# A fused attention, MLP and top-1 expert kernel: the first expert's rows from six gathered tiles and three tiles put to their slots by products, two low weight halves made later, another issue table

## The chip, the cores and the metric

The kernel runs on one core of one Trainium2 chip. The metric is device time in microseconds for one execution, lower is better. The runs shown are the median of three, with the lowest and the highest.

## The reference

```python
def _attn_ref(q, k, v, w1, b1, w2):            # B, H, S, D = 2, 8, 576, 64
    scores = scale * np.matmul(q, k.transpose(0, 1, 3, 2))
    x = (np.log1p(np.abs(rel)) / np.log1p(np.maximum(pos[:, None], 1.0)))[..., None]
    bias = np.maximum(x @ w1 + b1, 0.0) @ w2    # 32 hidden units, one bias per head
    attn = softmax(scores + bias.transpose(2, 0, 1)[None])
    return np.matmul(attn, v)

def _moe_ref(x, w_in, w_out):                   # x 1152x512, w_in 512x2048, w_out 2048x512
    h = x @ w_in
    return (h * np.tanh(np.log1p(np.exp(h)))) @ w_out

def _moe2_ref(x, w_gate, w1, w2, capacity):     # 8 experts, 512 -> 1024 -> 512, capacity 288
    expert_idx = np.argmax(x @ w_gate, axis=1)
    gate_w = softmax(x @ w_gate)[np.arange(N), expert_idx]
    # tokens go to their expert in the order of their numbers, until its 288 slots are full
    h = np.maximum(np.einsum('ecd,edf->ecf', disp, w1), 0.0)
    y = np.einsum('ecf,efd->ecd', h, w2)
    # out[i] = gate_w[i] * y[expert_idx[i], pos[i]] for the tokens kept, else 0
```

## The kernel before, in words

The program has two phases. **Phase 1** computes attention, the dense MLP and the gate. The 1152 tokens (2 batches of 576) are cut into five row tiles: `it` = 0 to 3 hold 128 rows of each batch (token tiles t = 0 to 7, two for each `it`), and `it` = 4 holds the 64 rows that are left of each batch (t = 8). For each row tile the scores, the bias of the relative positions, the exponentials and the product with v give the input planes PX of the MLP; `mlp_a` (products at L835 into banks of two hidden blocks, the gate function and its f16 high and low planes, L849 and L850) and `mlp_b` (products at L868, for `it` = 4 at L872) give y. Products of float accuracy are made of three f16 products: high by high, high by low, low by high.

`emit_y(it)` follows: `y_out` normalizes y (L942, L950), stores it to a scratch array `yscr` in memory, transposes it and makes the gate's logits (L964, L969); `rank_of` makes the argmax, the token's rank within its expert (one-hot rows o3, a product with a triangle at L1040) and writes token and weight to the slot table `tbl` by an indirect DMA on POOL (L1054). `slots(t)` adds one-hot rows times token numbers into `acc`, from which the rows of the first expert are read.

The first expert is the expert of token 0, known early, so that it needs no table: `first_rows` (after `it` = 3) turns `acc` into row numbers gid (L1133 to the tensor_scalar behind it), gathers the rows of the first expert from `yscr` in three groups of 96 slots (L1144, POOL) and splits them in f16 planes (L1148 high, L1149 low). `first_loads` loads its weights, measures their size and makes the f16 halves of W1 in four chunks (L1277 high, a L310 row with tile W low). `first_slots` puts rows to their slots by products: a diagonal dg moves the gathered rows (L1180), a marker tile of t = 8 moves the last tile's rows straight from the chip (L1184), for four column blocks and two planes, eight banks in all; each is cast to xT (L1186). 22 products that nobody reads stand ahead of them (L1170).

Nothing in phase 1 is issued where it is written. Each operation is recorded by `op(engine, cost, function, reads, writes, alternatives)`, and the table `ORDER` lists the operations by number (times 8, plus the way: an operation that may go to ScalarE or VectorE is sent to one of them by it). Buffers of the shared rings (R2: ra and rw, RB: pb and ps) are chosen when an operation is issued. DMAs go out on SP's queue in that order, indirect ones on POOL's. Each engine works off its own queue in order.

**Phase 2** is written in its order: `experts_list` (VectorE, list of the experts that have tokens), `gemm1(0)` and then, for each expert k, `gemm2(k)`, `gemm1(k + 1)`. `gemm1` makes eight hidden blocks ft, 12 products each (4 chunks ct by 3 planes, L1443), in four banks; each bank is taken by a Relu to the high plane HH (L1444, ScalarE) and a subtraction to the low plane (a L310 row with HH, VectorE); for ft = 2 to 5 the halves of W2 are made between them (L1427 and a L310 row with tile W). `gemm2` makes four blocks dt of 24 products (L1480) in two banks PY; between them stand the squares of the next expert's weights (L1213), their sum (L1216) and its f16 halves, and the next expert's rows, gathered at L1409. L307, L310, L313 and L327 are helpers (tensor_scalar, scalar_tensor_tensor, a scaled activation, a reduction) that many operations use.

## Time and profile before

| | us |
|---|---|
| median of the runs (n = 3) | 535.68 |
| lowest, highest | 534.3, 538.29 |
| the profiled execution | 534.81 |
| its span in the trace | 532.9 |

Its mean granted clock is 0.969 of full speed. TensorE is busy for 92% of the span, VectorE for 81%, ScalarE for 74%. The span is what lies between the first and the last instruction of the profiled execution; the time of the execution is 1.9 us longer. Times in a timeline are in us from the start of the span. PE is the matmul engine (TensorE), PEld its weight loads, DVE VectorE, ACT ScalarE, POOL GpSimd, SP the engine that issues most DMAs. PEclk is the clock that TensorE was granted, as a share of its full one. In a timeline row, what stands in brackets is how long the engine stood idle before the row, and what ended that.

### The profile page before, as it was taken

Reading aid. Unit: us, or ns where it says so; the run is one execution under the profiler, and the core shown is the slowest. Engines: PE = TensorE matmul, PEld = TensorE weight load, DVE = VectorE, ACT = ScalarE, POOL = GpSimd, SP = SyncE. Lnnn points to the kernel's source line nnn. Section 1 sums busy time; section 2 is a strip of 40 time slices with the busy share of each in tenths; the row PEclk is TensorE's granted clock in tenths of the full one; section 3 lists DMA queues with packets and bytes.
Section 4 is the critical chain, followed back from the end, with each engine's and each line's share of the span. In section 5 each row is a group of like instructions: output and inputs, shape, how many; then the busy total and the mean of one; then the engine's idle time right before and its main releaser. Section 6 shows DMA issues by size and latency. Waiting matters only on the chain.

```text
span 532.9 us, 11895 instructions
## 1 busy us (share of the span) xinstructions
PE 492.6 (92%) x4479; PEld 335.6 (63%) x4479; DVE 432.4 (81%) x1171; ACT 394.2 (74%) x808; POOL 37.8 (7%) x67
## 2 busy tenths in 40 slices
PE   4856988999999999999999999999999699999995
PEld 3411655676767674456687855899558478787551
DVE  7989899999987899999878874689988885869300
ACT  7989999999876899999996753366873357868210
POOL 1000010000000011000000000001001311212101
PEclk9896699999999999999999999999999899999999
DMA  8998787630010132346540112063001347695100
GB/s 313 414 366 293 234 290 260 228 129 1 12 63 1 66 132 68 112 152 211 169 122 5 50 35 58 21 230 128 2 26 47 105 134 237 218 342 188 42 15 19
DMA packets 28211, 73.78 MB, mean 138 GB/s; under 512 B 4838, under 2 KB 4966, under 8 KB 26096
## 3 DMA queue, kind: packets, MB, share of 16 engines
q1 hardware_dynamic: 26576, 69.21, 37.5%
q0 software_dynamic: 1568, 3.72, 2.4%
q8 instruction: 37, 0.61, 0.5%
q14 instruction: 30, 0.25, 0.2%
HBM read 55.27 MB, written 17.87 MB: 137 GB/s over the span
## 4 chain that ended last, share of the span: by engine, by line
PE 57%; DMA 19%; DVE 13%; ACT 7%; issue 3%; POOL 0%; SPq 0%; POOLq 0%; DVEq 0%; ACTq 0%
PE pb L868 16%; PE pb L835 12%; DMA out<-OC,tid 10%; PE pb L727 6%; DMA xg<-yscr,gid 6%; PE ps L835 6%; PE pb L663 3%; DMA rw<-wi 3%; PE pb L518 3%; PE ps L633 3%; PE ps L663 2%; ACT ra L655 2%; DVE rw L310 2%; ACT ra L666 2%; DVE rw L307 1%
## 5 line engine op out<-in xcount | busy, mean ns | idle before, releaser
L835 PEld LDWEIGHTS <-WIt 128*128 128x128 f16 x960 | 85.2, 98 | 10.6 <-issue 1.0
L835 PE MATMUL pb<-PX,WIt 128*128 128x256 f16 (+1 forms) x648 | 69.0, 263 | 0.0
L868 PE MATMUL pb<-WOt,ra 128*128 128x512 f16 x204 | 48.1, 379 | 0.0
L518 PE MATMUL pb<-ra,w2s 128*32 128x512 f32 (+17 forms) x252 | 37.0, 519 | 8.4 <-ACT rbe L532 3.7
L868 PE MATMUL pb<-WOt,rw 128*128 128x512 f16 x180 | 42.0, 380 | 0.0
L655 ACT ACTIVATE ra<-ra,rm 128x576 f32<-128x576 f32 x50 | 39.2, 788 | 2.2 <-DVE rm L654 1.8
L507 ACT ACTIVATE ra<-AT,stab 128x512 f32<-128x512 f32 (+17 forms) x62 | 38.4, 658 | 2.1 <-DVE stab L307 2.0
L310 DVE SCALAR_TENSOR_TENSOR W<-AT,wsc,W 128x1024 f16<-128x1024 f32 x24 | 30.5, 1279 | 6.1 <-ACT W L1427 5.8
L868 PEld LDWEIGHTS <-ra 128*128 128x128 f16 x204 | 19.8, 98 | 22.2 <-issue 0.9
L1443 PEld LDWEIGHTS <-W 128*128 128x128 f16 x288 | 28.1, 98 | 8.9 <-DVE W L310 1.2
L654 DVE CUSTOM_DVE_ANT_0 ra<-ps,ra 128x576 f32<-128x576 f32 x43 | 31.4, 753 | 2.7 <-PE ps L622 1.6
L727 PE MATMUL pb<-ra,AT 128*64 128x128 f32 (+1 forms) x540 | 32.7, 272 | 0.7 <-ACT ra L666 0.7
L835 PE MATMUL ps<-PX,WIt 128*128 128x256 f16 (+1 forms) x312 | 32.8, 260 | 0.0
L868 PEld LDWEIGHTS <-rw 128*128 128x128 f16 x180 | 17.3, 98 | 20.4 <-issue 1.4
L727 PEld LDWEIGHTS pb<-ra,AT 128*64 128x64 f32 x540 | 28.0, 139 | 3.3 <-issue 1.5
L532 ACT ACTIVATE rbe<-pb,rl 128x48 f32<-128x48 f32 (+25 forms) x64 | 28.5, 481 | 2.1 <-DMA bscr<-rbe 1.4
L1054 POOL DMA_INDIRECT tbl<-pk,rm x9 | 11.2, 1244 | 264.9 <-DVE rm L1051 175.8
L310 DVE SCALAR_TENSOR_TENSOR rw<-rw 128x1024 int32<-128x1024 int32 x24 | 29.1, 1215 | 0.0
L663 PE MATMUL pb<-ident,ra 128*128 128x128 f32 x159 | 24.0, 286 | 3.3 <-ACT ra L655 2.7
L666 ACT COPY ra<-pb 128x384 f32<-128x384 f32 x49 | 22.5, 492 | 3.5 <-PE pb L663 2.9
L1480 PE MATMUL py<-HH,W 128*128 128x288 f16 x192 | 24.7, 286 | 0.0
L307 DVE TENSOR_SCALAR ra<-AT,stab 128x544 f32<-128x544 f32 (+16 forms) x56 | 23.1, 443 | 0.9 <-PE pb L868 0.8
(477 smaller groups left out, 1151.7 us busy)
## 6 DMA issues: line engine op xcount, KB each, us to landing
AT<-m SPq DMA_DIRECT2D x24, 512.0 KB, 5.5
bscr<-rbe SPq DMA_DIRECT2D x36, 295.5 KB, 3.2
rw<-wo SPq DMA_DIRECT2D x8, 1024.0 KB, 5.4
ra<-bscr SPq DMA_DIRECT2D x28, 288.0 KB, 4.4
rw<-wi SPq DMA_DIRECT2D x4, 1024.0 KB, 9.2
WOt<-wi SPq DMA_DIRECT2D x4, 1024.0 KB, 8.5
AT<-k SPq DMA_DIRECT2D x4, 576.0 KB, 6.2
out<-ra SPq DMA_DIRECT2D x9, 256.0 KB, 2.6
```

Of the source, the lines that this page charges most:

```text
L307: eng.tensor_scalar(out=out, in0=in0, scalar1=s1, scalar2=s2, op0=op0, op1=op1)
L310: (eng or dve).scalar_tensor_tensor(out=out, in0=in0, scalar=s, in1=in1, op0=op0, op1=op1)
L507: on_act = lambda h_=h_, g=g: act.activation(h_.t[:, 0:dn], T[:, 0:dn], AF.Relu, bias=stab[:, g:g + 1])
L518: pe.matmul(ps.t[32 * c:32 * c + 32, 0:d1 - d0], w2s, hs[c].t[:, d0:d1], start=True, stop=True)
L532: op("ACT", c_act(n, 1, 50), lambda ends=ends: act.activation(*ends(), AF.Copy, scale=rl[:, blk:blk + 1]), r=[ps, "stab"], p=[be], alt=[(" ...
L654: op("DVE", c_dve(S), lambda i=i, own=own, m_=m_, b_=b_: dve.tensor_tensor_reduce(out=own(), in0=blk(s_.t[:, 960 * i:960 * i + S]), in1=bl ...
L655: op("ACT", c_act(S, 2), lambda i=i, m_=m_, col=col: act.activation(t_.t[:, S * i:S * i + S], t_.t[:, S * i:S * i + S], AF.Exp, bias=m_.t[ ...
L663: pe.transpose(pa.t[:, P * j:P * j + P], t_.t[:, 384 * n + P * j:384 * n + P * j + P], ident)
L666: op("ACT", c_act(384, 0, 55), lambda dst=dst, src=src: act.copy(dst(), src()), r=[pa], w=[("tT", it, ct, b, n)], hold=[t_], alt=[("DVE", ...
L727: pe.matmul(ov[64 * i:64 * i + 64, ct % 2, w * bb:w * bb + w], v_, t_.t[:, at + c0:at + c0 + w], start=n == 0, stop=n == 4)
L835: pe.matmul(ps.t[:, n * f_:n * f_ + n], WI[:, wv, ct, P * ft:P * ft + P], xt.t[:, xv, ct, 0:n], start=i == 0, stop=i == 11)
L868: pe.matmul(y_.t, gv()[:, g2, c:c + P], WO[:, wv, ft], **kw)
```

## The change

1. Another `ORDER`, with nine operations more.
2. The first expert's gather uses token tiles 0 to 5 alone: `first_rows` stands behind `it` = 2, and the count of rows goes over six tiles. Slots of t = 6 and 7 are not added to `acc`.
3. Tiles 6 and 7 (`it` = 3) get f16 planes on the chip (`planes`: a cast on ScalarE or VectorE and a subtraction on VectorE, L932 and L933), and their stores to `yscr` wait for the three gathers. Their rows and those of tile 8 are put to their slots by products with marker tiles m6, m7, m8: 24 products of 288 columns (L1199) instead of 8, besides the 24 of 96 columns with the diagonal (L1207). m7 takes in n0, the number of batch 0's rows in tiles 6 and 8, so one product and one VectorE operation more. `yscr` is zeroed where the gather may read rows not yet written.
4. 12 products that nobody reads (L1193) instead of 22, which wait for other things.
5. The low halves of W1's chunks 2 and 3 are made in phase 2, behind `experts_list`.
6. `gemm1(0)`: six banks (PH, PT and PY, those of the second product); 10 of 12 products of hidden blocks 0 to 5 first, without the low halves 2 and 3, then the two that are left of each, with Relu and subtraction behind each block; blocks 6 and 7 whole. For k > 0 the order is as before but for the loop's form.

```diff
@@ y_out
-            dma(lambda: yscr[t0:t0 + P], yv, 262144, r=[y_], p=["yscr"])
+            dma(lambda: yscr[t0:t0 + P], yv, 262144, r=[y_] + ([("g0", c) for c in range(NCH)] if it == NIT - 1 else []), p=["yscr"])
...
+            if it == NIT - 1:
+                planes(y_, yv)
@@
+    def planes(y_, yv):
+        h_ = pl.buf(R2)
+        hv = lambda v: h_.t.bitcast(F16)[:, DM * v:DM * v + DM]
+        op("ACT", c_act(DM), lambda: act.copy(hv(0), yv()), r=[y_], w=[h_], alt=[("DVE", c_dve(DM, 0.52), lambda: dve.tensor_copy(hv(0), yv()), 1)])
+        op("DVE", c_dve(DM), lambda: dve.tensor_tensor(out=hv(1), in0=yv(), in1=hv(0), op=ALU.subtract), r=[y_], w=[h_], lk=1)
+        yx.append((h_, hv))
@@ emit_y
-        if it == NIT - 1:
+        if it == NIT - 2:
             first_rows()
@@ first_slots
         def unread():
-            for i in range(22):
+            for i in range(12):
                 pe.matmul(pz.t[:, 0:SL], one, sl16, start=True, stop=True)
...
+                put = lambda i, m_, ps=ps, cc=cc, v=v: pe.matmul(ps.t[:, 0:SL], yx[i][1](v)[:, cc], m_.t.bitcast(F16)[:, 0:SL], start=i == 0, stop=i == 2)
+
+                def early(put=put):
+                    put(0, m6)
+                op("PE", 125, early, r=[yx[0][0], m6], w=[ps])
+
+                def f(ps=ps, cc=cc, v=v, put=put):
                     for c in range(NCH):
...
+                    put(1, m7)
...
+                op("PE", 125, lambda put=put: put(2, m8), r=[yx[2][0], m8], w=[ps])
@@ first_loads
-            op("DVE", c_dve(F2, 1.04, 1), lambda i=i, hi=hi: stt(W[1][:, 1, i], R1[:, i], sc(), hi(), ALU.mult, ALU.subtract), r=["W1", "R1", ("size", 0), ("W1h", i)], w=[("W1l", i)], lk=1)
+            if i < 2:
...
@@ gemm1
-        for ft in range(8):
-            ps = (PH + PT)[ft % 4]
-            for i, (ct, wv, xv) in enumerate([(ct, wv, xv) for ct in range(4) for wv, xv in P3]):
-                pe.matmul(ps[:, 0:SL], W1[:, wv, ct, P * ft:P * ft + P], XT[k % 2][:, xv, ct], start=i == 0, stop=i == 11)
+        banks = PH + PT if k else PH + PT + PY
...
+        ahead = 0 if k else len(banks)
+        for ft in range(ahead):
+            first(ft, [(ct, wv, xv) for wv, xv in P3 for ct in range(4) if not wv or ct < 2], True, False)
+        for ft in range(8):
+            ps = banks[ft % len(banks)]
+            if ft < ahead:
+                first(ft, [(ct, 1, 0) for ct in (2, 3)], False, True)
+            else:
+                first(ft, [(ct, wv, xv) for ct in range(4) for wv, xv in P3], True, True)
             act.activation(HH[:, 0, ft], ps[:, 0:SL], AF.Relu)
@@ phase 2
     experts_list()
...
+    for i in 2, 3:
+        stt(W1[:, 1, i], raw(0, i), sca(0, 0, 5), W1[:, 0, i], ALU.mult, ALU.subtract)
```

On POOL, the end of phase 1: the gathers of the first expert's rows (yscr, gid) among the writes of the slot table (tbl; pk_158 to pk_166 are tiles 0 to 8). Before:

```order
L1054 DMA tbl<-pk_163,rm_124 2304x2
L1054 DMA tbl<-pk_164,rm_123 2304x2
L1054 DMA tbl<-pk_165,rm_117 2304x2
L1144 DMA rw_105<-yscr,gid_183 96x512
L1144 DMA ra_112<-yscr,gid_183 96x512 x2
L1054 DMA tbl<-pk_166,rm_126 2304x2
```

And now:

```order
L1063 DMA tbl<-pk_163,rm_123 2304x2
L1160 DMA rw_105<-yscr,gid_183 96x512 x2
L1160 DMA ra_114<-yscr,gid_183 96x512
L1063 DMA tbl<-pk_164,rm_127 2304x2
L1063 DMA tbl<-pk_165,rm_118 2304x2
L1063 DMA tbl<-pk_166,rm_126 2304x2
```

The three gathers have moved ahead of the table writes of tiles 6 and 7.

On VectorE, the end of phase 1, up to the casts of the slots (xT) and the first operation of experts_list (A from cnt). W_4566 is W1 in f16, sl the slot numbers, rm a tile's slots. Before:

```order
L1149 TENSOR_TENSOR ra_109<-ra_112,ra_109 96x512
L307 TENSOR_SCALAR rm_126<-rm_126,e0s 128x1
L307 TENSOR_SCALAR rw_105<-sl_173,rm_126 128x288
L310 SCALAR_TENSOR_TENSOR W_4566<-AT,wsc,W_4566 128x1024 x2
L1186 CAST xT_4560<-pb_142 128x288
L1186 CAST xT_4560<-pb_141 128x288
L1186 CAST xT_4560<-ps_3923 128x288
L1186 CAST xT_4560<-pb_144 128x288
L307 TENSOR_SCALAR A<-cnt 1x8
```

And now, from the diagonal (ident, smsk) and m7 (with n_180) on:

```order
L1183 TENSOR_TENSOR ra_114<-ident,smsk 96x288
L1367 COPY cnt<-ps_3826 1x8
L307 TENSOR_SCALAR rw_105<-sl_173,rm_127,n_180 128x288
L310 SCALAR_TENSOR_TENSOR ra_111<-pb_143,rw_104,ra_111 128x512
L307 TENSOR_SCALAR rm_126<-rm_126,e0s 128x1
L307 TENSOR_SCALAR rw_106<-sl_173,rm_126 128x288
L1211 CAST xT_4517<-ps_3826 128x288
L1211 CAST xT_4517<-pb_141 128x288
L1211 CAST xT_4517<-pb_144 128x288
L1211 CAST xT_4517<-ps_3824 128x288
L307 TENSOR_SCALAR A<-cnt 1x8
```

The two low halves between the marker of tile 8 and the casts are gone, and so are the planes of the gathered rows; the marker m7 and tile 8's low plane stand there.

On VectorE, the start of phase 2, from the end of experts_list (lst) on; HH are the low planes of the hidden blocks by their banks, the W tile of the HH rows (W_5211, W_5181) is W2. Before:

```order
L1370 CAST lst<-fl 1x10
L307 TENSOR_SCALAR hm<-tok 96x1 x2
L310 SCALAR_TENSOR_TENSOR HH<-ph_5215,HH 128x288
L310 SCALAR_TENSOR_TENSOR HH<-ph_5216,HH 128x288
L310 SCALAR_TENSOR_TENSOR HH<-pt_5221,HH 128x288
L310 SCALAR_TENSOR_TENSOR W_5211<-AT,wsc,W_5211 128x1024
```

And now:

```order
L1396 CAST lst<-fl 1x10
L307 TENSOR_SCALAR hm<-tok 96x1 x2
L310 SCALAR_TENSOR_TENSOR W_4523<-AT,wsc,W_4523 128x1024 x2
L310 SCALAR_TENSOR_TENSOR HH<-ph_5185,HH 128x288
L310 SCALAR_TENSOR_TENSOR HH<-ph_5186,HH 128x288
L310 SCALAR_TENSOR_TENSOR HH<-pt_5191,HH 128x288
L310 SCALAR_TENSOR_TENSOR W_5181<-AT,wsc,W_5181 128x1024
```

The two low halves of W1 (W_4523) stand between the list of experts and the first low plane.

## Rows read from the trace of the kernel before

**Rows 1.** Windows by stage: length, busy PE, PEld, DVE, ACT, POOL, PEclk, DMA, GB/s.

```profile
0.00:103.30 103.30, 78.17 (x692) 44.37 (x693) 95.52 (x214) 96.46 (x193) 5.10 (x36) 0.88 0.83 298
103.30:397.60 294.30, 293.24 (x2797) 202.77 (x2794) 255.71 (x712) 232.19 (x496) 8.96 (x8) 1.00 0.25 84
397.60:412.90 15.30, 14.33 (x244) 13.22 (x243) 12.80 (x70) 5.83 (x13) 1.94 (x2) 1.00 0.19 63
412.90:429.30 16.40, 11.10 (x98) 7.77 (x98) 14.99 (x51) 6.24 (x14) 4.51 (x4) 0.79 0.29 85
429.30:441.10 11.80, 11.78 (x97) 9.42 (x98) 9.67 (x34) 7.01 (x11) 2.78 (x3) 1.00 0.57 190
441.10:455.40 14.30, 14.21 (x122) 11.60 (x119) 8.02 (x19) 12.33 (x21) 1.20 (x1) 1.00 0.78 243
```

**Rows 2.** ACT by line and shape, 0 to 101.6 us: count, busy us, mean ns, idle.

```profile
L655 ACT ACTIVATE ra<-ra,rm 128x576 f32<-128x576 f32 x19 | 15.2, 805 | 1.4 <-DVE rm L654 1.3
L666 ACT COPY ra<-pb 128x384 f32<-128x384 f32 x24 | 11.3, 506 | 0.0
...
L757 ACT ACTIVATE rw<-rw 128x1024 f32<-128x1024 f32 x4 | 4.7, 1185 | 0.0
...
L655 ACT ACTIVATION_READ_ACCUMULATOR ra<-ra,rm 128x1 f32 x19 | 4.2, 223 | 0.0
...
L532 ACT ACTIVATE rbe<-pb,rl 128x512 f32<-128x512 f32 x4 | 2.7, 680 | 0.0
...
L313 ACT ACTIVATE PX<-ra,xin 128x256 f16<-128x256 f32 x4 | 2.1, 530 | 0.0
```

**Rows 3.** Timeline, gate of tile 8 to t0: start us, us, engine, line, operation, tiles.

```profile
415.47 0.17 DVE L993 TENSOR_REDUCE rr<-pb 128x1 f32<-128x8 f32 x1
...
417.31 4.53 PE L1170 MATMUL pb<-sl,one 128*128 128x288 f16 x22
...
420.96 0.40 DVE L1148 CAST rw<-rw 96x512 f16<-96x512 f32 x1
421.40 0.69 DVE L1149 TENSOR_TENSOR rw<-rw,rw 96x512 f16<-96x512 f32 x1
...
425.12 0.29 DVE L307 TENSOR_SCALAR rw<-sl,rm 128x288 f16<-128x288 f16 x1
425.33 2.47 DVE L310 SCALAR_TENSOR_TENSOR W<-AT,wsc,W 128x1024 f16<-128x1024 f32 x2
```

**Rows 4.** Windows of the slot products' stretch, columns as in rows 1.

```profile
418.00:419.00 1.00, 1.00 (x6) 0.63 (x5) 1.00 (x1) 1.00 (x2) 0.79 (x1) 0.50 0.56 139
...
422.00:424.00 2.00, 0.25 (x2) 0.15 (x2) 1.86 (x8) 0.00 (x0) 0.00 (x0) 1.00 0.35 78
...
425.00:426.00 1.00, 0.99 (x13) 0.99 (x14) 0.96 (x3) 0.00 (x0) 0.00 (x0) 0.50 0.89 342
```

**Rows 5.** Timeline behind t0, columns as in rows 3.

```profile
429.32 3.11 PE L1443 MATMUL ph<-xT,W 128*128 128x288 f16 x24 [0.68 <-DVE A L307]
...
431.12 0.41 ACT L1444 ACTIVATE HH<-ph 128x288 f16<-128x288 f32 x1 [2.31 <-PE ph L1443]
...
432.05 0.19 DVE L307 TENSOR_SCALAR hm<-tok 96x1 f32<-96x1 int32 x2
...
434.25 1.14 ACT L1427 ACTIVATE W<-AT,wsc 128x1024 f16<-128x1024 f32 x1
...
435.42 1.28 DVE L310 SCALAR_TENSOR_TENSOR W<-AT,wsc,W 128x1024 f16<-128x1024 f32 x1 [0.58 <-ACT W L1427]
...
441.09 6.04 PE L1480 MATMUL py<-HH,W 128*128 128x288 f16 x48
...
441.44 0.81 DVE L310 SCALAR_TENSOR_TENSOR HH<-pt,HH 128x288 f16<-128x288 f32 x2
```

**Rows 6.** One line, the gathers L1144: durations in ns, and issue to landing.

```profile
L1144 POOL DMA_INDIRECT ra<-yscr,gid x2: 918/1288/1657, 417.0 to 418.2; - x2
...
DMA to landing us min/median/max: 3.0/3.6/3.8
```

More of the change, by code (lines that the diff above doesn't have):

```diff
@@ L1062, in emit_y @@
         for t, _ in rs:
-            m_ = slots(t)
-        if it == NIT - 1:
+            sm.append(slots(t))
+        if it == NIT - 2:
             first_rows()
@@ L1115, in f @@
             for b in range(2):
-                for t in range(b, 8, 2):
-                    pe.matmul(pn.t[:, E * b:E * b + E], one, o3[:, t, 1], start=t == b, stop=t == b + 6)
-        op("PE", 320, f, r=["rc0", "rc1"] + [("oh", t) for t in range(8)], w=[pn])
+                for t in range(b, 6, 2):
+                    pe.matmul(pn.t[:, E * b:E * b + E], one, o3[:, t, 1], start=t == b, stop=t == b + 4)
+        op("PE", 240, f, r=["rc0", "rc1"] + [("oh", t) for t in range(6)], w=[pn])
         def f():
@@ L1439, in gemm1, with first @@
             gather(k + 1)
-        for ft in range(8):
-            ps = (PH + PT)[ft % 4]
-            for i, (ct, wv, xv) in enumerate([(ct, wv, xv) for ct in range(4) for wv, xv in P3]):
-                pe.matmul(ps[:, 0:SL], W1[:, wv, ct, P * ft:P * ft + P], XT[k % 2][:, xv, ct], start=i == 0, stop=i == 11)
+        banks = PH + PT if k else PH + PT + PY
+        def first(ft, seq, a_, b_):
+            for i, (ct, wv, xv) in enumerate(seq):
+                pe.matmul(banks[ft % len(banks)][:, 0:SL], W1[:, wv, ct, P * ft:P * ft + P], XT[k % 2][:, xv, ct], start=a_ and i == 0, stop=b_ and i + 1 == len(seq))
+        ahead = 0 if k else len(banks)
+        for ft in range(ahead):
+            first(ft, [(ct, wv, xv) for wv, xv in P3 for ct in range(4) if not wv or ct < 2], True, False)
+        for ft in range(8):
+            ps = banks[ft % len(banks)]
[3 more added lines that the diff above has]
+                first(ft, [(ct, wv, xv) for ct in range(4) for wv, xv in P3], True, True)
             act.activation(HH[:, 0, ft], ps[:, 0:SL], AF.Relu)
```

48 lines of the change are left out of this document (29 added, 19 removed), and 218 rows, old and new, of the table ORDER.

## The prediction

> **What bounds the kernel now.** I read the windows by stage first [rows 1]. The reader is to see five different limits. Up to 103.3 us VectorE (95.5 us busy) and ScalarE (96.5) are full and TensorE, 78.2 busy, waits for them: the start is bounded by the work that these two have ahead of the first dense products. From 103.3 to 397.6 TensorE is busy for 293.2 of 294.3 us, so nothing done on another engine in that stretch moves the end, unless it stops TensorE. From 397.6 to 412.9 TensorE still has 14.3 of 15.3 us of products of the last row tile, with the gates of tiles 6 and 7 between them. From 412.9 to 429.3 it has 11.1 of 16.4 us, much of that products that nobody reads, at a mean granted clock of 0.79, while VectorE is busy for 15.0: this is the gate of the last tile and the filling of expert 0's slots, and VectorE leads. From 429.3 to 455.4 TensorE is full again (11.78 of 11.8, 14.21 of 14.3): expert 0's two products and expert 1's preparation.
>
> So three places can move the end: when the dense products start, how long it takes from the last tile's gate to the first product of expert 0 (I call that moment t0; before it is 429.32), and whether TensorE still goes without a pause from t0 on. I then read the sums by shape on ScalarE ahead of the first dense products [rows 2], the timeline from the gate to t0 [rows 3], the clock in single microseconds [rows 4] and the timeline behind t0 [rows 5].
>
> **The start.** The new table changes what stands ahead of the first tile's last input plane. Counted in the order of both kernels up to that plane, ScalarE has one exponential more (0.805 us, and its accumulator read of 0.22), one more of the 1024-wide quantizing activations L757 (1.19), about 0.85 more of bias evictions L532 (one of 352 and one of 191 columns for one of 16; I scale from 0.68 for 512 columns), two high planes less (2 x 0.53 = 1.06) and two copies L666 less (1.01); the L507 tiles are others of the same kind, +0.3 [rows 2]. That is 0.3 + 1.0 + 1.2 + 0.85 - 1.06 - 1.01, about +1.3 us on an engine that is busy for 96.5 of 103.3 [rows 1]. VectorE gets about +0.7. I take +1.3 us for the start. What the trace can't show is how the new order meshes: ScalarE idles 6.8 us in that stretch, and if half of this is saved or lost, the term goes to -2.1 or +4.7. The wider zeroing of the scratch rows (two stores of 393 KB for two of 131 KB) lies in a stretch where the DMA engines are 83% busy; its rows are not needed before the gather at some 390 us, so I count it at nothing; uncovered it would cost what 0.5 MB takes at the 298 GB/s of that row, 1.8 us, which lies inside the bound.
>
> **The long stretch.** TensorE gets six small products earlier (the marks' gather of rows, a few tenths of a us). VectorE has some 5 us more work there (two planes by subtraction, 0.69 each by the like rows; more operations given to it), ScalarE about the same. Both have gaps there: VectorE 255.7 busy of 294.3 [rows 1]. I count +0.0; the cover is TensorE's own queue of products.
>
> The first expert's gather now runs in this stretch. On POOL its three issues stand ahead of the table writes of tiles 6, 7 and 8 instead of behind those of 6 and 7; each issue costs POOL 0.9 to 1.7 us, about 1.2, and lands 3.0 to 3.8 us later [rows 6]. SP's queue gets a wait: the stores of tiles 6 and 7 wait for the three gathers, and behind them on SP stand the stores of tile 8, the output tiles and the read of the slot table, which before went out at 428.8; a gather that is back by some 400 us leaves all of them early. The six-tile gather's casts and subtractions (0.40 and 0.69 [rows 3]) go to VectorE and ScalarE among the last tile's planes. By TensorE's 14.3 us of products in the 15.3 us stage, which stay, the last product of the last tile comes at about the same distance: I take +0.2 (0 to +0.5).
>
> **From the gate to t0.** Before, the gate's first VectorE row is at 415.47 and t0 13.85 us later [rows 3]. What leaves this stretch on VectorE: the two W1 low halves just ahead of the slot casts (2.47), one of the earlier W1 low halves (1.24 by the same row), and the planes of the gathered rows, three subtractions of 0.69 and two casts of 0.40 (2.87): 6.6 us. What comes: the two marks of tiles 6 and 7 (about 0.3 each, as the mark of tile 8 at 425.12), their slot subtraction and n0's extra operation (0.2 each): 1.0. The last mark ended at 425.12 + 0.29, 9.9 us behind the gate, with 4.1 of those 6.6 us ahead of it: 9.9 - 4.1 + 1.0 = 6.8, and I add 1.0 for two short trips to TensorE and back that the removed rows covered. VectorE is then done 7.8 us behind the gate, and the diagonal about 1.4 us sooner, at 6.4. Then TensorE: 24 products of 96 columns and 24 of 288, four of which need only tile 6 and stand ahead. At full clock (24 x 130 = 3.11 us for a bank of 24 [rows 5]) it keeps up, and what is left behind the last mark is about nine products and one cast, 1.25 + 0.45: t0 at 9.5, a gain of 4.3. At half clock TensorE paces it from the diagonal on: 24 x 0.08 + 20 x 0.26 + 0.45 = 7.6, t0 at 14.0, a gain of -0.1. The rows stand nearer to neither: before, the fillers 417.31 to 421.84 took 206 ns each with the clock granted at 0.50 in 418 to 419, and the slot products ran at 0.50 too in 425 to 426 [rows 4], after two microseconds (422 to 424) in which TensorE was busy for 0.25 us; 0.50 is the lower of its two levels, 1.2 of 2.4 GHz. I take the middle, a gain of 2.1. What is late next is TensorE's slot products.
>
> By the Trainium skill, page "TensorE: Matmul & The Clock Gate", section "Part 1: The HAM clock gate (the "warmup" mystery)", the throttled clock is the default and activity is what releases it. This trace agrees: 0.50 stands behind sparse rows and 1.00 behind full ones. The rule speaks against having 12 unread products in place of 22; by it alone the gain would be the -0.1.
>
> **Expert 0.** This term goes the wrong way. Before, TensorE finishes one bank of the first product (12 matmuls, 1.5 us) after another, and ScalarE and VectorE start on the hidden rows 1.8 us behind t0 (431.12 [rows 5]). After, TensorE does 10 of 12 products of six banks first, 60 matmuls, then two for bank 0: the first bank is whole after 62 x 0.123 us + 0.3, 7.9 us behind t0 (0.123 is 96 matmuls from 429.32 to 441.09). All that ScalarE and VectorE do with expert 0 then begins 6 us later: eight high planes and four W2 high halves on ScalarE (8 x 0.41 + 4 x 1.14 = 7.8), eight low planes and four W2 low halves on VectorE (8 x 0.41 + 4 x 1.28 + 0.5 = 8.9) [rows 5]. VectorE starts behind the first high plane, 8.3, and ends at 17.2 without a wait; with about 1 us of waits for the high halves, 18.3. Before it was 442.25 - 429.32 = 12.9. TensorE can begin the second product earlier (its first bank is that of hidden block 4, free at 14.5 or so), but the last two matmuls of its first bank need the last low plane: 18.8, where before it was 14.8 (441.09 + 3.0). The second bank, 3.0 us on, ends at 21.9 instead of 17.8, and everything of expert 1 stands behind it (its scale, then its products). The loss is 4.1 us, by the waits 3.0 to 5.0. What the reordering buys, that W1's low halves 2 and 3 (2.47) come behind the list of experts (done 432.24 [rows 5]), is already in the gain above: they fit in the 7.9 us, so they cost nothing new. The loads of expert 1's W1 chunks 2 and 3 go to the same memory and wait on SP for them; they are wanted by the squares L1213, which stand behind expert 0's last high plane on ScalarE, some 10 us later: hidden.
>
> **The sum.** +1.3 + 0.2 - 2.1 + 4.1 = +3.5 us. The profiled execution took 534.81 us (span 532.9), so 538.3. The median of the runs shown is 535.68, 0.9 above that; I leave the forecast at 538.3, since the runs of before spread over 4 us. About 1% (5.4 us) is what a measurement can tell from no change: faster means under 530.3, slower over 541.0. The ends together: -2.1 + 0 - 4.3 + 3.0 = -3.4, and +4.7 + 0.5 + 0.1 + 5.0 = +10.3, so 531.4 to 545.1.
>
> **Rivals.**
> *The clock stays low through the slot products* (slower). With 10 unread products less, TensorE comes to them from a thinner stretch. For it: 0.50 in 425 to 426 after the thin stretch, even with 22 fillers [rows 4]. Against it: four slot products and the small gate products now stand early and thicken it. Price: the gain goes from 2.1 to -0.1 (2.2), and if the first ten of the 60 matmuls still take 0.206 instead of 0.123, 0.8 more: 541.3. It decides when 0.50 stands in the windows at t0.
>
> *VectorE stops in front of a gathered block* (slower, and the mechanism is a queue). Its casts and subtractions now stand ahead of the last tile's planes and of the gates of tiles 6 and 7 on the same in-order engine. From the row index on VectorE to the third block's landing I count 3 x 1.2 + 3.8 = 7.4 us and the step to POOL, some 8 [rows 6]; by like rows VectorE has about 7 us of work before the first of these rows and 10 before the third. If the index or POOL is late by a landing, 3.8 us go to the last tile's products: 542.1. It decides from a delay of about 2 us on; against it, the first two blocks land earlier.
>
> *An early start and a full clock* (faster side). If the new table saves half of ScalarE's idle time in the start (-2.1 instead of +1.3) and VectorE alone paces the slots (4.3 instead of 2.1), the time is 538.3 - 3.4 - 2.2 = 532.7. For it: both idle times are in the rows; against it, ScalarE has more work ahead, not less.
>
> **How the numbers follow.** The forecast has 0.63, the clock 0.13, the stopped VectorE 0.10, the early start 0.14. Of the forecast's share 0.08 lies over 541.0 and 0.03 under 530.3 (misjudged waits behind t0); of the clock's 0.08 lies over 541.0, the rest just below, of the stopped VectorE's all; of the early start 0.05 lies under 530.3. That makes slower 0.26, faster 0.08, within 1% 0.66. The range 531.5 to 545.0 takes in all four and nearly the ends of the terms.
>
> **What would show it.** In the changed kernel's profile: the first dense product between 101 and 108 us, and TensorE full from there to the last 512-wide product; the gate's first VectorE row some 11.5 us ahead of t0, with no W1 low half between; and behind t0 about 8 us without a hidden plane on ScalarE, then TensorE waiting for several us in the second product's first bank for VectorE's low planes. If TensorE shows no such wait, the largest term is wrong; if the first dense product moves by more than 4 us, the term with the least behind it decides the result.

## The result

The changed kernel took 530.64 us (median of 12 runs, 529.62 to 534.56) where the kernel before took 535.68 (12 runs beside it, 534.29 to 538.29): a ratio of 0.9914, 95% interval 0.9894 to 0.9933. It is 0.9% faster, about 4.6 us. I had forecast 538.3, 2.6 us or 0.5% slower, with a range from 531.5 to 545.0. A second comparison gave 0.9918 (0.9892 to 0.9943). All ratios below leave out one execution, of b_lowfirst2, that took 647.6 us at a mean granted clock of 0.745.

The profiled execution of the changed kernel took 531.95 us, its span is 530.0, 2.9 less than before. The windows by stage, with the columns of [rows 1]:

```profile
0.00:101.20 101.20, 73.67 (x692) 40.44 (x693) 95.96 (x217) 96.39 (x191) 5.35 (x37) 0.90 0.84 303
101.20:396.60 295.40, 293.50 (x2808) 203.43 (x2807) 263.84 (x728) 232.28 (x494) 10.28 (x10) 1.00 0.28 89
396.60:410.50 13.90, 13.71 (x236) 13.13 (x234) 12.11 (x55) 6.39 (x16) 1.30 (x2) 1.00 0.10 36
410.50:423.40 12.90, 10.60 (x100) 7.65 (x101) 9.86 (x51) 5.53 (x13) 2.16 (x2) 0.74 0.21 62
423.40:435.00 11.60, 11.60 (x95) 9.22 (x96) 7.85 (x30) 3.71 (x8) 0.00 (x0) 1.00 0.52 178
435.00:450.00 15.00, 12.94 (x110) 10.40 (x109) 10.56 (x22) 13.38 (x23) 3.94 (x3) 1.00 0.72 216
```

TensorE starts its full stretch 2.1 us earlier, with ScalarE as busy as before (96.39 us) in less time. VectorE has 9.9 us of work in the gate's window where it had 15.0. And TensorE, full behind t0 before, now has 2.1 us of pauses in 435 to 450: what the reordering of expert 0's first product gives back.

The table sets the stages of all kernels of this study side by side, each from one profile: the start of the first dense product (L835), from there to the end of the last product of the last row tile (L872), to the gate's first VectorE row, to t0, from t0 to the small product with the size of expert 1's W1 (the one behind the second bank of expert 0's second product), from there to the first of the last products, and the end. Each number is the length of a stage in us.

| kernel | start | to last L872 | to gate | to t0 | to scale | to last products | to end | span |
|---|---|---|---|---|---|---|---|---|
| before | 103.3 | 309.6 | 2.6 | 13.8 | 17.9 | 72.0 | 13.7 | 532.9 |
| before, again (before2) | 103.1 | 309.6 | 2.6 | 13.8 | 17.9 | 72.0 | 13.7 | 532.7 |
| changed | 101.2 | 309.0 | 2.3 | 10.9 | 20.1 | 72.8 | 13.7 | 530.0 |
| changed, again (after2) | 101.4 | 310.5 | 2.3 | 9.6 | 20.1 | 72.9 | 13.9 | 530.7 |
| a_oldgemm | 102.0 | 309.0 | 2.3 | 9.6 | 24.4 | 73.3 | 13.8 | 534.2 |
| a_lowfirst2 | 101.5 | 309.3 | 2.3 | 9.6 | 18.3 | 73.3 | 13.8 | 528.0 |
| a_low_fill16 | 100.6 | 309.0 | 2.3 | 11.0 | 18.2 | 72.0 | 13.8 | 526.8 |
| a_fill6 | 100.5 | 310.1 | 2.3 | 11.4 | 20.1 | 73.2 | 13.9 | 531.3 |
| a_fill22 | 102.6 | 309.0 | 2.3 | 10.1 | 20.1 | 73.2 | 13.7 | 530.9 |
| a_bstart | 102.5 | 310.8 | 2.0 | 11.0 | 20.1 | 73.2 | 13.8 | 533.3 |
| b_astart | 101.2 | 318.0 | 2.7 | 13.8 | 19.4 | 73.3 | 13.8 | 542.3 |
| b_late | 102.3 | 311.0 | 2.1 | 14.0 | 21.8 | 73.2 | 13.8 | 538.1 |
| b_lowfirst2 | 102.5 | 309.6 | 2.1 | 14.0 | 18.8 | 73.3 | 13.8 | 534.0 |
| b_low_fill40 | 102.0 | 309.8 | 2.1 | 12.7 | 18.2 | 72.0 | 13.8 | 530.5 |

How the start went, ScalarE by line and shape up to the first dense product, columns as in [rows 2]:

```profile
L655 ACT ACTIVATE ra<-ra,rm 128x576 f32<-128x576 f32 x20 | 15.9, 804 | 0.0
...
L757 ACT ACTIVATE rw<-rw 128x1024 f32<-128x1024 f32 x5 | 6.0, 1190 | 0.0
```

The exponential and the quantizing activation more that I had counted are there; both are also there by the end of ScalarE's last input plane (100.37), the moment at which [rows 2] stops. But the 1.4 us that the 19 exponentials of before waited, nearly all for VectorE [rows 2], are gone: ScalarE stands idle for 4.8 us of the start instead of 6.8.

The timeline from the gate (412.49) to t0, columns as in [rows 3]:

```profile
412.49 0.15 DVE L1002 TENSOR_REDUCE rr<-pb 128x1 f32<-128x8 f32 x1
...
414.25 3.06 PE L1193 MATMUL pb<-sl,one 128*128 128x288 f16 x12
...
417.39 0.17 DVE L1178 TENSOR_TENSOR nb<-pb,oh 128x8 f32<-128x8 f32 x1 [0.81 <-PE pb L1174]
...
418.42 0.45 DVE L1183 TENSOR_TENSOR ra<-ident,smsk 96x288 f16<-96x288 f32 x1
...
420.02 0.29 DVE L307 TENSOR_SCALAR rw<-sl,rm 128x288 f16<-128x288 f16 x1
421.73 0.46 DVE L1211 CAST xT<-ps 128x288 f16<-128x288 f32 x1 [1.42 <-PE ps L1199]
...
422.85 0.46 DVE L1211 CAST xT<-ps 128x288 f16<-128x288 f32 x1
...
423.36 2.62 PE L1470 MATMUL ph<-xT,W 128*128 128x288 f16 x20 [0.55 <-DVE A L307]
```

The last marker ends 7.8 us behind the gate, as forecast, the diagonal 6.4, as forecast, and t0 comes 10.9 behind it. VectorE waits 0.81 us for a small product that stands behind the 12 unread ones, which took 3.06 us here, and its first cast waits 1.42 us for TensorE's slot products.

The timeline behind t0, columns as in [rows 5]:

```profile
426.22 2.46 DVE L310 SCALAR_TENSOR_TENSOR W<-AT,wsc,W 128x1024 f16<-128x1024 f32 x2
...
431.30 0.71 ACT L1481 ACTIVATE HH<-ph 128x288 f16<-128x288 f32 x2 [8.17 <-DMA AT<-m]
...
434.84 1.17 ACT L1453 ACTIVATE W<-AT,wsc 128x1024 f16<-128x1024 f32 x1
...
436.64 1.27 DVE L310 SCALAR_TENSOR_TENSOR W<-AT,wsc,W 128x1024 f16<-128x1024 f32 x1
436.82 2.49 PE L1517 MATMUL py<-HH,W 128*128 128x288 f16 x19 [1.48 <-ACT HH L1481]
...
437.84 0.45 DVE L310 SCALAR_TENSOR_TENSOR HH<-py,HH 128x288 f16<-128x288 f32 x1
...
439.40 0.81 DVE L310 SCALAR_TENSOR_TENSOR HH<-ph,HH 128x288 f16<-128x288 f32 x2
439.90 3.71 PE L1517 MATMUL py<-HH,W 128*128 128x288 f16 x29 [0.58 <-DVE HH L310]
```

The first hidden plane comes 7.9 us behind t0, as forecast. TensorE waits 1.48 us to begin the second product and 0.58 us for the last low planes, which end at 440.2, 16.9 us behind t0 (forecast: 18.3).

### The profile page after: what moved, and what is told of

Same layout as the page of the kernel before. It is cut to its first block, busy times and chain, and to the rows that moved or that the text cites. A ratio compares the mean times of both kernels' runs of the same rounds, so it can differ in the third digit from the quotient of the medians.

```text
span 530.0 us, 11936 instructions
## 1 busy us (share of the span) xinstructions
PE 487.4 (92%) x4484; PEld 331.9 (63%) x4484; DVE 437.4 (83%) x1177; ACT 393.3 (74%) x805; POOL 36.5 (7%) x67
## 4 chain that ended last, share of the span: by engine, by line
PE 58%; DMA 20%; DVE 12%; ACT 6%; issue 3%; POOL 1%; SPq 0%; POOLq 0%; DVEq 0%; ACTq 0%
PE pb L868 16%; PE pb L835 12%; DMA out<-OC,tid 10%; PE pb L727 6%; DMA xg<-yscr,gid 6%; PE ps L835 4%; PE pb L663 3%; PE ps L633 3%; PE pb L518 3%; DMA WOt<-wi 2%; PE ps L663 2%; PE ps L619 2%; PE pb L872 2%; DVE ra L654 1%; DVE rw L310 1%
## 5 line engine op out<-in xcount | busy, mean ns | idle before, releaser
L835 PEld LDWEIGHTS <-WIt 128*128 128x128 f16 x960 | 85.0, 98 | 10.7 <-issue 1.8
L835 PE MATMUL pb<-PX,WIt 128*128 128x256 f16 (+1 forms) x720 | 76.5, 262 | 0.0
L868 PE MATMUL pb<-WOt,ra 128*128 128x512 f16 x276 | 63.0, 379 | 0.0
L868 PEld LDWEIGHTS <-ra 128*128 128x128 f16 x276 | 26.7, 98 | 30.1 <-issue 0.9
L507 ACT ACTIVATE ra<-AT,stab 128x448 f32<-128x448 f32 (+17 forms) x63 | 39.3, 666 | 2.1 <-DVE stab L307 1.4
L518 PE MATMUL pb<-ra,w2s 128*32 128x512 f32 (+16 forms) x236 | 31.4, 523 | 4.7 <-ACT rbe L532 2.0
L532 ACT ACTIVATE rbe<-pb,rl 128x512 f32<-128x512 f32 (+46 forms) x56 | 26.4, 500 | 1.9 <-PE pb L518 1.9
L619 PE MATMUL ps<-AT,rq 64*128 64x512 f32 x64 | 20.0, 703 | 6.6 <-DMA AT<-k 5.4
L835 PE MATMUL ps<-PX,WIt 128*128 128x256 f16 (+1 forms) x240 | 25.9, 262 | 0.0
L868 PE MATMUL pb<-WOt,rw 128*128 128x512 f16 x108 | 25.4, 379 | 0.0
L663 PEld LDWEIGHTS pb<-ident,ra 128*128 128x128 f32 x171 | 19.2, 144 | 6.9 <-ACT ra L655 3.5
```

Of the source, the lines that this page charges most:

```text
L507: on_act = lambda h_=h_, g=g: act.activation(h_.t[:, 0:dn], T[:, 0:dn], AF.Relu, bias=stab[:, g:g + 1])
L518: pe.matmul(ps.t[32 * c:32 * c + 32, 0:d1 - d0], w2s, hs[c].t[:, d0:d1], start=True, stop=True)
L532: op("ACT", c_act(n, 1, 50), lambda ends=ends: act.activation(*ends(), AF.Copy, scale=rl[:, blk:blk + 1]), r=[ps, "stab"], p=[be], alt=[(" ...
L619: pe.matmul(s_.t[r, 1024 * i:1024 * i + 512], q_.t[hs, c], kraw[hs, k0 + 576 * bb:k0 + 576 * bb + 512], start=True, stop=True)
L663: pe.transpose(pa.t[:, P * j:P * j + P], t_.t[:, 384 * n + P * j:384 * n + P * j + P], ident)
L835: pe.matmul(ps.t[:, n * f_:n * f_ + n], WI[:, wv, ct, P * ft:P * ft + P], xt.t[:, xv, ct, 0:n], start=i == 0, stop=i == 11)
```

## The experiments

Names beginning with a_ are edits of the changed kernel, with b_ of the kernel before. Their ratios are to the kernel before on the same chip, in alternation. The changed kernel's own ratio, 0.9914 and 0.9918, is what the a_ kernels are held against; only a_low_fill16 ran beside the changed kernel itself. The expectations of the last comparison count "gate to t0" from the gate's second VectorE row, some 0.45 us later than the table does.

**a_oldgemm: expert 0's first product in the order of before.**

```diff
-        banks = PH + PT if k else PH + PT + PY
+        banks = PH + PT
-        ahead = 0 if k else len(banks)
+        ahead = 0
```

> The changed kernel with expert 0's first product in the order of before (12 products bank by bank in four banks); the two low halves of W1 still come behind the list of experts. Theory 1 (the reordering pays for the late halves but gives some of it back, since the hidden planes begin late): TensorE now waits in the first bank for the low halves 2 and 3, which end some 5.3 us behind t0; the first bank is whole at about 5.5 us behind t0 instead of 7.9, the eight banks end at about 16.5, the second product's second bank at about 22.3 instead of 20.0: some 2 us slower than the changed kernel, 532.5 to 533. Theory 2 (what holds the second product is only the run of hidden planes on VectorE and ScalarE, 9 us from the first whole bank on): those begin 2.4 us earlier, so it would be up to 2 us faster than the changed kernel, 528.5.

Ratio 0.9974 (0.9957 to 0.9991): some 3 us slower than the changed kernel. Theory 1 has the direction, and its price was too small: t0 to scale is 24.4, where it had 22.3 for the end of the second bank. Its timeline:

```profile
422.81 1.15 PE L1470 MATMUL ph<-xT,W 128*128 128x288 f16 x8 [0.55 <-DVE A L307]
...
426.98 0.90 PE L1470 MATMUL ph<-xT,W 128*128 128x288 f16 x3 [3.02 <-DVE W L310]
...
428.18 3.30 PE L1470 MATMUL ph<-xT,W 128*128 128x288 f16 x13 [0.29 <-DVE W L310]
```

TensorE stops at the ninth product for 3.0 us and at the twelfth once more, and gets nothing back. With late low halves the reordering is worth 4.3 us in the profile and some 3 in the runs; so the reordering is no error of the change, it is what makes the late halves bearable.

**a_lowfirst2: the low halves behind the casts at once, ahead of the list of experts, and two banks ahead.**

```diff
     table(0)
+    for i in 2, 3:
+        stt(W1[:, 1, i], raw(0, i), sca(0, 0, 5), W1[:, 0, i], ALU.mult, ALU.subtract)
     experts_list()
-    for i in 2, 3:
-        stt(W1[:, 1, i], raw(0, i), sca(0, 0, 5), W1[:, 0, i], ALU.mult, ALU.subtract)
...
-        banks = PH + PT if k else PH + PT + PY
+        banks = PH + PT
-        ahead = 0 if k else len(banks)
+        ahead = 0 if k else 2
```

> The changed kernel with the two low halves of W1 between the slot casts and the list of experts, and only two banks done ahead in expert 0's first product (four banks in all). Theory 1: the low halves end 2.4 us behind t0, just when 20 matmuls are done; the first hidden plane comes at 3.0 us behind t0 instead of 7.9, TensorE runs without a pause, and the second product's second bank ends at 17.9 instead of 20.0: about 2 us faster than the changed kernel, 528.5. Theory 2 (the list of experts, 2.5 us later, sets when expert 1's weights arrive, and these are what is late): no gain or a loss, a wait for the load of AT ahead of the squares of expert 1's weights.

Ratio 0.9882 (0.9866 to 0.9898), 1.7 us under the changed kernel by ratios whose intervals still touch; a_low_fill16 below, which ran beside the changed kernel, makes the gain clear. Theory 1 holds: t0 to scale falls from 20.1 to 18.3, and TensorE goes through:

```profile
422.63 3.11 PE L1470 MATMUL ph<-xT,W 128*128 128x288 f16 x24 [0.55 <-DVE xT L1211]
...
425.66 0.71 ACT L1481 ACTIVATE HH<-ph 128x288 f16<-128x288 f32 x2 [3.27 <-DVE t L1382]
...
434.67 6.04 PE L1517 MATMUL py<-HH,W 128*128 128x288 f16 x48
...
440.92 0.49 PE L1241 MATMUL po<-ident,wsc 128*128 128x128 f32 x2 [0.21 <-DVE wsc L327]
```

The first hidden plane comes 3.0 us behind t0, the second product's 48 matmuls go without a pause, and the later list of experts leaves 0.21 us of a wait at the scale.

**a_fill6 and a_fill22: 6 and 22 unread products instead of 12.**

```diff
-            for i in range(12):
+            for i in range(6):
```

> The changed kernel with 6 unread products instead of 12. Theory 1 (the unread products hold up the count of the last tile's rows, two small products behind them on TensorE, for which VectorE waited 0.8 us): that wait goes, t0 comes up to 0.8 us earlier, 530. Theory 2 (they hold the clock up): the granted clock stays at 0.50 longer, the slot products take twice as long, t0 comes 1 to 2 us later, 532.

> The changed kernel with 22 unread products, as before. Theory 1 (they stand in the way): ten more at 0.21 to 0.25 us are 2 to 2.5 us ahead of the count of the last tile's rows, VectorE waits, t0 comes some 1.5 to 2.5 us later, 532.5. Theory 2 (they hold the clock up and the clock is what decides): the slot products run at 1.00 from the first on, t0 no later or up to 1 us earlier.

With 6 the ratio is 0.9951 (0.9937 to 0.9966), slower than the changed kernel; with 22 it is 0.9926 (0.9908 to 0.9944), no different. Single microseconds of a_fill6, columns as in [rows 1]:

```profile
414.00:415.00 1.00, 0.98 (x15) 0.86 (x15) 0.86 (x7) 0.38 (x1) 0.00 (x0) 1.00 0.03 1
415.00:416.00 1.00, 0.32 (x4) 0.20 (x3) 0.90 (x8) 1.00 (x5) 0.00 (x0) 0.60 0.00 0
416.00:417.00 1.00, 0.19 (x2) 0.13 (x2) 0.93 (x8) 1.00 (x2) 0.00 (x0) 0.50 0.55 121
...
421.00:422.00 1.00, 1.00 (x10) 0.73 (x9) 0.00 (x0) 0.00 (x0) 0.00 (x0) 0.50 0.04 14
```

with the first cast of the slots behind them:

```profile
422.57 0.46 DVE L1211 CAST xT<-ps 128x288 f16<-128x288 f32 x1 [2.82 <-PE ps L1199]
```

and single microseconds of a_fill22:

```profile
416.00:417.00 1.00, 1.00 (x10) 0.80 (x9) 0.90 (x8) 1.00 (x4) 0.00 (x0) 1.00 0.00 0
...
420.00:421.00 1.00, 1.00 (x17) 0.89 (x17) 0.96 (x4) 0.00 (x0) 0.00 (x0) 1.00 0.73 271
```

With 6, TensorE is nearly empty from 415 to 417, the granted clock falls to 0.50 and the slot products run at it until 422: gate to t0 11.4. With 22 the clock stays at 1.00 and t0 comes at 10.1, 0.5 later than the 9.6 that the changed kernel's code has at full clock, since ten products more stand ahead of the small one. Both theories of each pair have a part. In a_fill6 VectorE did get the 0.8 us of theory 1: its last marker ends 6.9 us behind the gate instead of 7.8 (after2 below, with 12 at full clock, has 6.9 too). But its first cast then waits 2.82 us for slot products at half clock. That the clock decides in the runs too is likely and not shown: the six runs of a_fill6 have mean granted clocks of 0.968 to 0.975, the 12 of the changed kernel 0.967 to 0.985.

**a_bstart and b_astart: the start of one table on the other kernel.** The table written out is what this comes to, with the first 450 entries of before's table (a_bstart) or the first 470 of the changed one (b_astart), in the numbers of the kernel itself:

```diff
+ORDER = first + [c for c in ORDER if c // 8 not in {x // 8 for x in first}]
```

> The changed kernel, its issue table beginning with the first 450 entries of before's table (in the numbers of this kernel), the rest in its own order: the start of before, the change behind it. Theory 1 (the 2.1 us by which the first dense product is earlier come from the order of the start): the first dense product is back at about 103 us, and the time 1.5 to 2.5 us longer, 532.5. Theory 2 (the gain has another source, or a late start is caught up in the full stretch): the first dense product stays at 101, or the time stays at 530.6.

> Before's kernel, its issue table beginning with the first 470 entries of the changed one (in before's numbers), the rest in its own order. Theory 1: the first dense product comes at about 101.2 us and the time is 1.5 to 2.5 us shorter than before, 533.5. Theory 2: what is early at the start is lost again, the end of the 512-wide products of the fourth row tile does not move, 535.7.

a_bstart: 0.9968 (0.9954 to 0.9983), 2.9 us slower than the changed kernel: theory 1, with somewhat more than its 1.5 to 2.5. Its first dense product is at 102.5; the stretch to the last L872 is 310.8, no clear loss, since the changed kernel's own profiles have 309.0 and 310.5. b_astart: 1.0162 (1.0135 to 1.0189), the start is at 101.2, and the stretch is 318.0 instead of 309.6. So the early start goes with the table's beginning, but before's kernel cannot take it over without a loss in the stretch behind it. In b_astart TensorE is busy for 46.2 of 50 us in 200 to 250, where before fills them; this is a result on the splice, and it doesn't price the start. The many profiles price it: the code of the changed kernel's start showed 100.5 to 102.6 in eight profiles (mean 101.4), that of before 102.0 to 103.3 in six (mean 102.6). The start is worth about 1.2 us, give or take 0.7 (two standard errors), and a single pair of profiles, 2.1 here, can't tell it better than to a microsecond. Part of the spread is a wait for the loads of the dense weights: VectorE waits 0.2 us for them (tile WOt) in a_fill6, whose start is 100.5, and 1.8 us in a_fill22, whose start is 102.6.

**b_late: before with the late low halves and six banks ahead; b_lowfirst2: before with the low halves behind the casts and two banks ahead.** The edits are parts 5 and 6 of the change (shown with the change), with two operations less in the table; b_lowfirst2 then has those of a_lowfirst2.

```diff
+            if i < 2:
...
+        ahead = 0 if k else len(banks)
```

> Before's kernel with two parts of the change alone: the two low halves of W1 behind the list of experts, and expert 0's first product with six banks ahead. Theory 1: t0 comes 2.0 to 2.5 us earlier (the casts stand behind the marker of the last tile at once, unless TensorE's products at half clock hold them), and 2.2 us are given back by the hidden planes: no difference from before, within 1 us. Theory 2 (my forecast's sum): t0 2.0 earlier at most and 4.1 given back: 2 us slower, 537.7.

> Before's kernel with the two low halves of W1 between the slot casts and the list of experts and two banks done ahead in expert 0's first product. Theory 1: t0 2.0 to 2.5 us earlier and nothing given back: 533.5. Theory 2: TensorE at half clock holds t0, or the later list of experts costs what is gained: 535 or more.

b_late: 1.0033 (1.0014 to 1.0052), 1.8 us slower. b_lowfirst2: 0.9996 (0.9979 to 1.0014). In both, gate to t0 did not get shorter: 14.0 where before has 13.8. But these edits take less off that stretch than the expectations say. Of the two low halves just ahead of before's casts only one belongs to chunks 2 and 3; the other of these stands ahead of the gate, at 406.89. In the edited kernels one low half, of chunk 1, still stands between the last marker and the casts. So 1.24 us of VectorE's work left the stretch from the gate to the casts, not 2.47. The other 1.24 left the time ahead of the gate, and the gate's first row comes 0.5 us sooner behind the last L872 (2.1 for 2.6). VectorE's row in before, and then its rows at the casts of b_lowfirst2:

```profile
406.89 1.28 DVE L310 SCALAR_TENSOR_TENSOR W<-AT,wsc,W 128x1024 f16<-128x1024 f32 x1
```

```profile
423.96 1.28 DVE L323 SCALAR_TENSOR_TENSOR W<-AT,wsc,W 128x1024 f16<-128x1024 f32 x1
425.87 0.94 DVE L1199 CAST xT<-pb 128x288 f16<-128x288 f32 x2 [0.63 <-PE pb L1197]
```

Single microseconds of b_lowfirst2, columns as in [rows 1]:

```profile
424.00:425.00 1.00, 1.00 (x15) 1.00 (x14) 1.00 (x2) 0.00 (x0) 0.00 (x0) 0.50 0.18 68
425.00:426.00 1.00, 1.00 (x7) 0.63 (x5) 0.37 (x2) 0.38 (x1) 0.00 (x0) 0.50 0.00 0
```

TensorE's slot products at 0.50 hold the casts, and VectorE now waits for them. In b_late the low clock goes on behind t0, where 20 products took 4.29 us; the changed kernel's 20 took 2.62:

```profile
429.32 4.29 PE L1458 MATMUL ph<-xT,W 128*128 128x288 f16 x20 [0.55 <-DVE xT L1199]
```

That is 1.7 of the 3.9 us by which its t0 to scale (21.8) is longer than before's. So parts 5 and 6 alone make the old kernel slower. That they pay only where TensorE's slot products are early is argued: no run has part 3, or the earlier gather, alone.

**before2, after2: both kernels once more. b_low_fill40: b_lowfirst2 with 40 unread products instead of 22.**

```diff
-            for i in range(22):
+            for i in range(40):
```

> Before's kernel once more, for a second profile on the chip of this comparison. Theory 1 (the first dense product's moment varies by about 1 us from profile to profile of the same code: five profiles of the changed kernel's start showed 100.5 to 102.6): 102.3 to 103.4. And the stretch from expert 1's first product to the last products, 63.8 in the first profile of before and 64.8 to 65.1 in all others, comes out at 65: it is no part of the change. Theory 2: both stay at 103.3 and 63.8, and the change did lengthen the end by 1 us.

> The changed kernel once more, beside the three others of this comparison. Theory 1: ratio 0.989 to 0.993 to before; gate to t0 is 9.1 us where the clock stays at 1.00 behind the unread products, 10.4 where it falls to 0.50, which the same code showed in different profiles. Theory 2 (the clock falls at the same place in every execution of this code): 10.4 again.

> Before's kernel with the low halves behind the casts and two banks ahead, which by itself gained nothing (t0 stayed 13.5 us behind the gate), and 40 unread products instead of 22, so that TensorE is busy until the planes of the gathered rows are there. Theory 1 (t0 was held by the slot products at a granted clock of 0.50, so what VectorE was relieved of did not count): the slot products run at 1.00, gate to t0 11.5 to 12, the time 1.5 to 2 us less than before. Theory 2 (VectorE or the gather holds t0): gate to t0 13.4, no gain.

before2 repeats before's profile within 0.2 us in every stage. The start is where theory 1 had it, the end where theory 2 had it: from the scale to the last products the changed kernel took 72.8 and 72.9, before 72.0 twice. This is not bound to the change, though: a_fill6, with the same code there, has 73.2 without the wait that the changed kernel shows (under *Behind it* below), and edits of the old kernel have 73.2 and 73.3. after2 has the clock at 1.00 where the first profile of the same code had 0.50, and gate to t0 is 9.6 instead of 10.9. The first profile's rows, then after2's:

```profile
415.00:416.00 1.00, 1.00 (x6) 0.64 (x5) 0.90 (x8) 1.00 (x4) 0.00 (x0) 0.50 0.00 0
...
418.00:419.00 1.00, 1.00 (x14) 0.58 (x13) 0.93 (x6) 0.00 (x0) 0.04 (x1) 0.50 0.91 256
```

```profile
416.00:417.00 1.00, 1.00 (x10) 0.80 (x9) 0.87 (x7) 0.99 (x4) 0.00 (x0) 1.00 0.00 0
...
418.00:419.00 1.00, 0.71 (x14) 0.56 (x14) 0.91 (x5) 0.51 (x1) 0.07 (x1) 1.00 1.04 297
```

after2's last marker ends 6.9 us behind the gate (414.24), where the first profile has 7.8:

```profile
420.86 0.30 DVE L307 TENSOR_SCALAR rw<-sl,rm 128x288 f16<-128x288 f16 x1
```

b_low_fill40: 0.9977 (0.9958 to 0.9997), gate to t0 12.7 instead of 14.0, and its slot products ran at 1.00:

```profile
424.00:425.00 1.00, 1.00 (x18) 0.87 (x15) 1.00 (x1) 0.36 (x2) 0.00 (x0) 1.00 0.44 143
```

That is theory 1, with 1.3 us in the profile for the 1.5 to 2 expected; in the runs it is about 1 us under b_lowfirst2, with intervals that overlap. The clock was part of what held t0 in the old kernel. The rest is VectorE's own queue, with the low half that stayed: the casts follow it without a wait, and TensorE waits for them.

```profile
423.81 1.28 DVE L323 SCALAR_TENSOR_TENSOR W<-AT,wsc,W 128x1024 f16<-128x1024 f32 x1
425.00 0.81 DVE L1199 CAST xT<-pb 128x288 f16<-128x288 f32 x2
426.61 3.11 PE L1458 MATMUL ph<-xT,W 128*128 128x288 f16 x24 [1.01 <-DVE xT L1199]
```

Between 12.7 in this kernel and 9.6 in the changed one, both at full clock, lie 3.1 us. They are not the price of the earlier gather alone: two low halves, this one and one at 416.29, some 2.4 us of VectorE, still stand between gate and casts here, and the new table makes both ahead of the gate.

**a_low_fill16: a_lowfirst2 with 16 unread products.**

```diff
-            for i in range(12):
+            for i in range(16):
```

> The changed kernel with the low halves 2 and 3 between the slot casts and the list of experts, two banks ahead in expert 0's first product, and 16 unread products instead of 12: they end just when the small product behind them could start anyway. Theory 1: 1.7 us less than the changed kernel from the hidden planes, and the clock at 1.00 through the slot products in most executions, gate to t0 9.1 to 9.3: 2 us less than the changed kernel, 528.5 to 529. Theory 2 (four more products only stand in the way): no better than the same kernel with 12, 0.988 of before.

Ratio 0.9878 (0.9852 to 0.9904), median 529.25, beside 531.77 of the changed kernel in the same comparison: 2.5 us less, and the best of the study. Theory 1's first part holds (t0 to scale 18.2). Its second part is not shown: in its own profile the clock stood at 0.50 from 414 to 417, under the unread products, which took 3.76 us; gate to t0 was 11.0, and against a_lowfirst2 (0.9882) there is no difference that can be measured.

## Why the prediction was wrong

Three terms missed to the same side, each by one to two and a half us. The first step that failed is the start, put at +1.3 and measured at -1.2 (mean): it counted ScalarE's work and put the change in the waits at nothing (its bounds, -2.1 to +4.7, allowed for them). The next is the size of expert 0's loss, 4.1 where 2.2 was measured, below its own lower bound of 3.0; and the gain up to t0 was taken as 2.1 where 3.0 and 4.3 were measured.

| term | forecast | profiles, first pair | what the runs showed |
|---|---|---|---|
| the start | +1.3 | -2.1 | -1.2 as a difference of means over fourteen profiles |
| the long stretch, to the gate | +0.2 | -0.9 | 309.0 and 310.5 against 309.6, and 0.3 less to the gate |
| gate to t0 | -2.1 | -3.0 | -3.0 at half clock, -4.3 at full clock |
| expert 0 | +4.1 | +2.2 | 20.1 against 17.9, in both profiles of each kernel |
| behind it | 0 | +0.9 | +0.9 in both pairs, but 72.0 to 73.3 with edits of either kernel |
| sum | +3.5 | -2.9 | |

*The start* failed, in its sign. "About +1.3 us on an engine that is busy for 96.5 of 103.3" took a sum of row durations for the delay, and the waits as given. Up to the end of its last input plane ScalarE is busy for 95.56 us (0 to 100.37) where it was 94.88 (0 to 101.72): 0.7 more, about half of what I counted. Its idle time up to there fell from 6.8 to 4.8 us. And what the first dense product follows, in both kernels by 0.2 us, is VectorE's last input plane; before, then changed:

```profile
102.25 0.86 DVE L310 SCALAR_TENSOR_TENSOR PX<-ra,xin,PX 128x256 f16<-128x256 f32 x2
```

```profile
100.14 0.89 DVE L310 SCALAR_TENSOR_TENSOR PX<-ra,xin,PX 128x256 f16<-128x256 f32 x2
```

VectorE's idle time up to there fell from 7.8 to 5.2 us. These two waits of before (total us, times, longest) are in neither list of the changed kernel's profile:

```profile
DVE ra L654 <- PE ps L622: 1.6, 2, 1.4
ACT ra L655 <- DVE rm L654: 1.3, 1, 1.3
```

Other waits grew and shrank; which of them carries the gain was not tried. It was the first half of my third rival, at 0.14, which I held unlikely because ScalarE had more work. That the first pair shows just its -2.1 is luck, since single profiles of one code differ by as much. An engine that is busy for 93% by the windows is not full, and a new table acts on the 7%.

*The long stretch* with the step to the gate came out 0.9 shorter in the first pair and 0.6 longer in the second, about the +0.2 forecast. TensorE is not quite full there: it waits once for VectorE, 1.7 us, in both profiles of the changed kernel. In after2 the clock fell to 0.50 behind that wait (0.83 on average in 110 to 120, 1.00 in the first profile), and its stretch is 1.5 us longer.

*From the gate to t0* the mechanism was right in what comes last: TensorE's slot products, for which VectorE's first cast waits 1.42 us. That VectorE was done at 7.8, as forecast, is partly luck: 0.81 of it is the wait for a small product behind unread products at half clock, and in after2 it was done at 6.9. There t0 came at 9.6 for the 9.5 forecast at full clock, since TensorE needed 2.6 us behind the last marker and not the 1.7 that I summed. The size lay outside the middle that I took: a gain of 3.0 at half clock in one profile and 4.3 at full clock in the other, against 2.1 with an end of -0.1 at half clock. That end was the step that failed. It put 7.6 us of slot products behind the diagonal; the first profile has 4.5, since seven slot products, not four, stood ahead of the diagonal's and the clock, at 0.50 from 413, was back at 1.00 by 420. Even a_fill6, with the clock at 0.50 until 422, has 5.9. Nor do the parts add up as gains of their own: in b_late and b_lowfirst2 1.2 us less of VectorE's work ahead of the casts gained nothing.

*Expert 0* had the right mechanism and was sized too large. I summed durations of rows, 7.8 us for ScalarE and 8.9 for VectorE, and added 1 us of waits. The trace shows that two neighbouring rows of an engine overlap: the last high planes end 6.7 us behind the first one's start (431.30 to 437.95), a high plane taking 0.29 of the queue where its row says 0.42, and a low half 1.20 (436.64 to 437.84) where its row says 1.27. VectorE's rows took 8.0 us, with 0.45 us of waits. So the last low plane came 16.9 us behind t0 and not 18.3: of these 1.4 us some 0.9 are the overlap and 0.5 the waits. The other 0.4 to 0.5 by which the term was too large lie behind it, where TensorE had less left to do than I counted.

The rivals: the low clock happened, in the first profile, at a price of 1.3 us and not 3, and it was over by 420, ahead of t0. VectorE in front of a gathered block did not: the three gathers left POOL from 392.64 on and landed in 3.2 to 3.8 us, and the first cast went at once:

```profile
398.83 0.20 DVE L307 TENSOR_SCALAR ra<-ra,gl 128x1 f32<-128x1 f32 x1
398.95 0.41 DVE L1164 CAST rw<-rw 96x512 f16<-96x512 f32 x1
```

*Behind it*, one new wait of TensorE, at expert 2's first product:

```profile
481.48 0.30 PE L1470 MATMUL ph<-xT,W 128*128 128x288 f16 x1 [0.90 <-DVE W L310]
```

VectorE is late there by a wait of 1.03 us, 5 us earlier, for the indirect write of output rows (476.30). That a_low_fill16, with the same gather and a shorter expert 0, hasn't this wait, and a_fill6, with the same code behind t0, hasn't it either, speaks for a collision in time; it was not tried by itself.

What stays open: the medians differ by 5.0 and 3.9 us in the two comparisons, the profiled executions by 2.9 and 2.0 (534.81 to 531.95, 534.6 to 532.65). Both profiled executions of the changed kernel lie 0.9 to 1.3 us above its median and both of before as much below theirs, so a microsecond or two of the gain is in no profile here; the clock's two courses and the start's spread are of that size, but that they make it up is only argued. For it: the first profiled execution had a mean granted clock of 0.970, and nine of the other eleven runs had 0.975 to 0.985. Against it: the second had 0.976, in the middle of its runs.

## What to carry to other kernels

Time queues by the distance from one start to the next, not by durations of rows, wherever an engine works without a pause; the sums here were 10% (VectorE) and 17% (ScalarE) too long. Before taking work off one engine, ask which engine is next: in the old kernel 1.2 us came off VectorE ahead of the casts and t0 did not move, because TensorE at half clock was just as late. And look up which operation a row is before counting on its removal: two neighbouring rows of the same form were taken for the same pair of halves, and one of them stayed. Last, work that is put off should be put behind the last thing that needs its engine and no further: the low halves directly behind the casts, with two banks done ahead (both were changed together), kept the early t0 and saved 1.7 us of what the six banks cost.
